# Sparse attention and an FFN on one core: in the last quarter VectorE transposes half of the weights in 32x32 blocks, and the rest of the transpose goes through DRAM

## The chip, the core and the metric

The kernel runs on one core of a Trainium2 chip. The core has a matrix engine (TensorE, PE in the profile; its weight loads are the row PEld), a vector engine (VectorE, DVE), a scalar engine (ScalarE, ACT), GpSimd (POOL) and a sync engine (SP) that issues most of the DMAs. Each engine works through its own list of instructions in order and waits for the others by semaphores. The metric is the device time of one execution in microseconds, lower is better.

## The reference

Attention with the 32 largest scores kept, over 8 batches of 8 heads, 576 positions and a head size of 64; then an FFN with an ELU. Cut to what matters:

```python
scores = q @ k.T / 8                       # (8, 8, 576, 576)
kth = the 32nd largest of each row
scores = where(scores >= kth, scores, -1e9)
attn = exp(scores - max); attn = attn / (attn.sum(-1) + 1e-9)
x = (attn @ v), heads side by side         # (4608, 512)
h = x @ w_in                               # (4608, 2048)
g = where(h > 0, h, exp(min(h, 0)) - 1)
out = g @ w_out                            # (4608, 512)
```

All of it is in float32; w_in and w_out come in as float64 and are decoded on the chip in the first steps.

## The kernel before

The attention is cut into 144 steps. A step is 128 queries of one batch and one pair of heads (or 64 remaining queries of two pairs), with all 576 keys: a score tile `sc` of 128 x 2 x 576. A batch has 18 steps: 16 ordinary ones and two for the remaining queries, which come last in an even batch and first in an odd one. Four ordinary steps (two remaining ones) make one tile of tokens over all eight heads.

What a step does, by engine: TensorE multiplies q and k (`scores`, L331, matmuls at L348) and ScalarE copies the product into `sc` (L368). VectorE looks for the 32nd largest value of each row: `first_max` (L373) finds eight, and three calls of `next_max` (L377) each replace the eight found (L379) and find the next eight (L385). GpSimd pushes the scores below the 32nd far down (`mask`, L397 to L399), ScalarE takes the exponential and its sum `den` (`exp`, L435). Then the weights have to be transposed so that TensorE can multiply them with v: `trans` (L464) makes nine TensorE transposes through PSUM (L475, eight, and L493, one), and ScalarE copies them into `et` (L480, L494). `attend` (L496, matmuls at L508) multiplies `et` with v into `av`. At the end of a tile, `invert` (L440) adds EPS to the sums (L444), takes the reciprocal (L445), transposes it in small (L446), and spreads it over the partitions by way of DRAM (L450, L456, L462); `normalise` (L520) multiplies with it on GpSimd (L523).

The steps overlap. In iteration n of the loop VectorE works on step n; mask and exponential belong to step n-1, the transpose to step n-2. In even iterations TensorE first computes the scores of step n+2, then attends for the steps n-4 and n-3, then computes the scores of step n+3. `et` has two buffers, one for even and one for odd steps; `sc` has seven. k and q of a step are loaded by `load_kq` (L328) from a DRAM copy of their transposed form, four steps ahead. That form is made once for each batch and pair of heads: the pairs 4 to 19 are loaded by `load_qk` (L228, L234), transposed by TensorE in the iterations that `turns` names (L682 to 686; `transpose_qk`, L299, L307) and stored by `keep_kq` (L322); the last twelve pairs are transposed by VectorE in 32x32 blocks (`transpose_blocks`, L264), in an order that the loads (`load_blocks`, L252, L255) have prepared.

The FFN is fed in pieces between these. The tokens are grouped into blocks of one to three tiles (`sizes`, L623, for each pair of batches). When the last tile of a block is normalised, its pieces join a queue: 32 pieces of the hidden layer (`hidden`, L536, matmuls at L543; ScalarE L557 to L559 and GpSimd L560 make the ELU) and eight for each tile of the projection (`project`, L562, matmuls at L567, copy out at L576, store at L579). `feed` (L600) is called twice in each iteration and issues pieces up to a share of planner's units a step; a piece of the projection counts 1.75, one of the hidden layer 1.33 for three tiles and 0.89 for two. The share is what is left divided by the steps until the next block is due, with a cap (L606): 6.6 in the first half of the steps, 7.2 in the second. What is left at the end is issued after the last step.

The first six steps (`EARLY`) run without this overlap: exponential, transpose, attend and normalise of step n-1 stand in iteration n, and the mask is made by another route (`mask_early`, L401, with the Relu of ScalarE at L423 and a subtraction at L426). In them and in the next few the weights of the FFN are decoded in `decode` slots (L661; VectorE L188 and L189, GpSimd L193, ScalarE L182 and L183).

The order of every engine's instructions is the order in which this program issues them.

Of the kernel before, what the change touches and what calls it, by code (L numbers as in the profile page):

```python
# [16 lines left out]
EPS = 1.0e-9  # L17
# [44 lines left out]
def kernel(  # L62
# [313 lines left out]

    def next_max(u, between=None):  # L377
        for i in range(2):
            nc.vector.match_replace(u.wk[:, i, :], u.m[:, i, :], u.cur[:, i, :], TAKEN)  # L379
        u.cur = u.wk  # L380
        if between is not None:
            decode(*between)
        u.m = small.tile([P, 2, 8], FP32, tag="m", name="m")
        for i in range(2):
            nc.vector.max(u.m[:, i, :], u.cur[:, i, :])  # L385
# [14 lines left out]

    def mask_early(u):  # L401

# [13 lines left out]
        for i in range(2):  # L416
            at = slice(i, i + 1)
            nc.gpsimd.tensor_scalar(
                pos[:, at], kth[:, at], neg[:, at], -1.0, ALU.mult, ALU.mult
            )  # L420
        for i in range(2):
            pen, s = u.wk[:, i, :], u.sc[:, i, :]
            nc.scalar.activation(  # L423
                pen, s, AF.Relu, scale=neg[:, i : i + 1], bias=pos[:, i : i + 1]
            )
            nc.gpsimd.tensor_tensor(s, s, pen, ALU.subtract)  # L426
        biases(u, True)

    def exp(u, i):
        g = u.g  # L430
        if g.den is None:
            g.den = small.tile([P, H], FP32, tag="den", name="den", bufs=2)
        at = u.hps[i] if g.rem else i * NHP + u.hps[0]
        s = u.sc[:, i, :]
        nc.scalar.activation(  # L435
            s, s, AF.Exp, bias=u.neg[:, i : i + 1], scale=scale,
            accum_out=g.den[:, at : at + 1],
        )

    def invert(g):  # L440


        n = NHP if g.rem else H
        nc.vector.tensor_scalar_add(g.den[:, 0:n], g.den[:, 0:n], EPS)  # L444
        nc.vector.reciprocal(rec[:, 0:n], g.den[:, 0:n])  # L445
# [18 lines left out]
    def trans(u):  # L464
# [27 lines left out]
        else:  # L492
            nc.tensor.transpose(ps[:, 0, 0:P], e[:, JP : JP + P], ident[:])  # L493
            nc.scalar.copy(half[:, 0, :], ps[:, 0, 0:P])  # L494

    def attend(u):  # L496
        u.attended = True
# [4 lines left out]
        for j, hp in enumerate(u.hps):  # L502
            for c in range(J + 1):
                for i in range(2):
                    r = slice(i * D, (i + 1) * D)
                    at = (j if g.rem else i) * J + c if c < J else 2 * J + j
                    q0 = (i ^ j) * R if g.rem else 0
                    nc.tensor.matmul(  # L508
# [91 lines left out]
    def feed(n, part):  # L600
# [4 lines left out]
        until = next(r for r in dues if r > n) - n  # L605
        share = min(left / until, 6.6 if n < NS // 2 else 7.2)  # L606

# [14 lines left out]
    EARLY = 6  # L622
    sizes = {0: (1, 1, 1, 1, 1, 1, 1, 2), 2: (2, 2, 2, 3), B - 2: (3, 3, 2, 1)}  # L623
    steps, first, order = [], {}, []
# [27 lines left out]
    for n, blk in enumerate(order):  # L652
        blk.over = order[n + 2] if n + 2 < len(order) else None
    NS = len(steps)
    dues = [blk.ready for blk in order] + [NS + 5]

    def sums(u):
        u.summed = True
        invert(u.g)
# [16 lines left out]
    for p, pair in enumerate(pairs):  # L676
# [6 lines left out]
        elif p >= NHP:  # L683
            n = p - 2 if p < NHP + 4 else p - 1
            n = n if n < EARLY + 5 else EARLY + 5 + 2 * (n - EARLY - 5)
            turns[n] = pair
# [18 lines left out]
    with tc.manual_schedule():  # L705
# [20 lines left out]
        for n in range(NS + 4):  # L726
# [39 lines left out]
            if early:  # L766
# [9 lines left out]
                feed(n, 0.5)  # L776
                if last and last.ends:
                    sums(last)
                next_max(now, (n, 3))
                decode(n, 4)  # L780
# [6 lines left out]
                next_max(now, (n, 5))  # L787
                if last and last.ends:
                    normalise(last.g)
                mask_early(now)  # L790
                decode(n, 6)
# [8 lines left out]
            if last:  # L800
                if n > EARLY:
                    mask(last, 1)
                exp(last, 0)
            if done and not done.turned:
                trans(done)
# [50 lines left out]
```

## Time and profile before

| | |
|---|---|
| median of 3 runs | 1649.95 us (1649.19 to 1651.17) |
| the profiled execution | 1647.37 us, of which its span 1644.3 |
| TensorE busy | 1577.9 us, 96% of the span |
| VectorE busy | 1476.5 us, 90% |
| GpSimd, ScalarE busy | 1142.4 and 914.2 us |
| transposes of the weights on TensorE (L475), 1152 | 151.4 us busy |
| their copies by ScalarE (L480), 144 | 144.7 us |
| DMA queue of SP and ScalarE | 166400 packets, 172.1 MB |

The span starts with the first instruction. A step starts on VectorE with its first MAX8 of L373: step 4 at 68.8 us, step 11 at 162.6, step 74 at 794.6, step 108 at 1152.4, and the last one, 143, at 1521.4. An ordinary step without waits takes VectorE 9.6 us. Durations in the profile are those of one instruction and neighbours overlap a little, so sums of steps are taken from start to start. Waits are put down to the instruction that came last.

### The profile page before, as it was taken

How to read it: one execution, taken by the hardware profiler on the slowest of the kernel's cores; microseconds unless marked ns; L12 is line 12 of the kernel's file. 1: busy time of each engine (PE TensorE's matmuls, PEld its weight loads, DVE VectorE, ACT ScalarE, POOL GpSimd, SP SyncE). 2: the span in 40 equal slices, each digit the busy share in tenths (PEclk: the TensorE clock that was granted, in tenths of full speed). 3: DMA queues.
4: the chain of work that ended last, by engine and by line, in shares of the span. 5: the costliest groups of instructions: out<-in, count | busy, mean ns of one | idle time of the engine just before them, and what ended most of it. 6: DMA issues, size and time to landing. Idle time of an engine off the chain costs nothing.

```text
span 1644.3 us, 28759 instructions
## 1 busy us (share of the span) xinstructions
PE 1577.9 (96%) x9928; PEld 1057.7 (64%) x9928; DVE 1476.5 (90%) x3098; ACT 914.2 (56%) x1865; POOL 1142.4 (69%) x1456
## 2 busy tenths in 40 slices
PE   7878999999999999999899999999999999999999
PEld 5665777777675858576565665565565565565565
DVE  7999799999999999999999999989999989989200
ACT  5875566555564646455464574565475475465221
POOL 3777677677786878777687687677687588678321
PEclk9979999999999999999999999999999999999999
DMA  9864454423131413233423524333433312120000
GB/s 312 267 196 130 138 176 141 134 88 118 31 122 46 154 57 115 71 93 92 120 68 104 173 72 128 110 84 107 121 94 118 132 51 89 68 71 14 20 7 13
DMA packets 168914, 174.52 MB, mean 106 GB/s; under 512 B 124225, under 2 KB 132417, under 8 KB 168769
## 3 DMA queue, kind: packets, MB, share of 16 engines
q1 hardware_dynamic: 166400, 172.10, 33.8%
q8 instruction: 78, 1.28, 0.3%
q10 hardware_dynamic: 2368, 0.59, 0.2%
q14 instruction: 68, 0.55, 0.1%
HBM read 144.18 MB, written 28.46 MB: 105 GB/s over the span
## 4 chain that ended last, share of the span: by engine, by line
PE 81%; POOL 6%; DVE 4%; ACT 3%; DMA 3%; issue 2%; SPq 1%; ACTq 0%; DVEq 0%; POOLq 0%
PE ops L567 28%; PE hps L543 27%; PE avps L508 9%; PE scps L348 9%; PE eps L475 6%; POOL sc L399 2%; DVE m L385 2%; DVE wk L379 1%; POOL wk L397 1%; POOL gT L560 1%; DMA w_out<-in_moe_w_in_dram 1%; POOL wk L398 1%; DMA kin<-in_k_dram 1%; PE qkps L299 1%; PE eps L493 1%
## 5 line engine op out<-in xcount | busy, mean ns | idle before, releaser
L385 DVE MAX8 m<-wk 128x8 f32<-128x576 f32 x864 | 609.1, 746 | 0.0
L543 PE MATMUL hps<-xT,w_in 128*128 128x128 f32 (+2 forms) x2432 | 535.3, 376 | 13.8 <-POOL xT L523 10.2
L567 PE MATMUL ops<-w_out,gT 128*128 128x512 f32 x1152 | 519.8, 596 | 8.3 <-ACT osb L576 8.3
L543 PEld LDWEIGHTS hps<-xT,w_in 128*128 128x128 f32 x2432 | 385.4, 195 | 138.8 <-issue 19.4
L379 DVE MATCH_REPLACE8 wk<-m,wk 128x576 f32<-128x576 f32 x576 | 423.1, 742 | 0.0
L399 POOL TENSOR_TENSOR sc<-sc,wk 128x576 f32<-128x576 f32 x276 | 389.1, 1410 | 23.0
L567 PEld LDWEIGHTS ops<-w_out,gT 128*128 128x128 f32 x1152 | 209.6, 190 | 243.0 <-issue 213.2
L435 ACT ACTIVATE sc<-sc,neg 128x576 f32<-128x576 f32 x288 | 224.1, 778 | 224.1 <-POOL sc L399 222.0
L560 POOL TENSOR_TENSOR gT<-gT,n 128x384 f32<-128x384 f32 (+1 forms) x168 | 187.6, 1121 | 180.8 <-ACT n L559 178.3
L368 ACT COPY sc<-scps 128x576 f32<-128x576 f32 x287 | 169.4, 641 | 115.4 <-PE scps L348 113.3
L397 POOL TENSOR_SCALAR wk<-sc,nth 128x576 f32<-128x576 f32 x276 | 206.2, 747 | 26.9
L379 DVE MATCH_REPLACE8 wk<-m,sc 128x576 f32<-128x576 f32 x288 | 211.6, 742 | 0.0
L373 DVE MAX8 m<-sc 128x8 f32<-128x576 f32 x288 | 200.8, 738 | 0.3 <-issue 0.2
L348 PE MATMUL scps<-kq 64*128 64x288 f32 (+3 forms) x1344 | 182.3, 420 | 19.4 <-ACT sc L368 9.3
L398 POOL TENSOR_SCALAR wk<-wk 128x576 f32<-128x576 f32 x276 | 184.0, 667 | 22.8
L480 ACT COPY et<-eps 128x1024 f32<-128x1024 f32 x144 | 144.7, 1005 | 76.8 <-PE eps L475 75.2
L508 PE MATMUL avps<-et,vE 128*64 128x128 f32 (+1 forms) x3200 | 175.5, 265 | 5.4 <-ACT et L480 3.4
L508 PEld LDWEIGHTS avps<-et,vE 128*64 128x64 f32 x3200 | 158.1, 137 | 32.2 <-issue 24.2
L475 PEld LDWEIGHTS eps<-ident,sc 128*128 128x128 f32 x1152 | 133.4, 141 | 56.4 <-issue 36.5
L557 ACT ACTIVATE n<-hps 128x384 f32<-128x384 f32 (+1 forms) x168 | 90.3, 537 | 136.7 <-PE hps L543 132.7
L348 PEld LDWEIGHTS scps<-kq 64*128 64x128 f32 (+1 forms) x1344 | 102.4, 176 | 88.9 <-issue 33.4
L475 PE MATMUL eps<-ident,sc 128*128 128x128 f32 x1152 | 151.4, 274 | 6.8 <-ACT sc L435 2.9
(73 smaller groups left out, 963.6 us busy)
## 6 DMA issues: line engine op xcount, KB each, us to landing
kq<-kqd SPq DMA_DIRECT2D x152, 576.0 KB
kqd<-kq SPq DMA_DIRECT2D x32, 576.0 KB
rb<-recd SPq DMA_DIRECT2D x64, 128.0 KB
out_dram<-osb SPq DMA_DIRECT2D x32, 256.0 KB
kin<-in_k_dram SPq DMA_DIRECT2D x18, 256.0 KB
qin<-in_q_dram SPq DMA_DIRECT2D x17, 256.0 KB
w_out<-in_moe_w_in_dram SPq DMA_DIRECT2D x2, 2048.0 KB
vE<-in_v_dram SPq DMA_DIRECT2D x32, 128.0 KB
```

The costliest lines, as they stand in the source:

```text
L348: nc.tensor.matmul(ps[rows, j, at : at + keys.stop - keys.start], u.kq[hp][r, 1, q0 : q0 + g.ql], u.kq[hp][r, 0, keys], start=True, stop=True,
L373: nc.vector.max(u.m1[:, i, :], u.sc[:, i, :])
L379: nc.vector.match_replace(u.wk[:, i, :], u.m[:, i, :], u.cur[:, i, :], TAKEN)
L385: nc.vector.max(u.m[:, i, :], u.cur[:, i, :])
L397: nc.gpsimd.tensor_scalar(pen, s, u.nth[:, i : i + 1], 2.0**100, ALU.add, ALU.mult)
L399: nc.gpsimd.tensor_tensor(s, s, pen, ALU.add)
L435: nc.scalar.activation(s, s, AF.Exp, bias=u.neg[:, i : i + 1], scale=scale, accum_out=g.den[:, at : at + 1],)
L475: nc.tensor.transpose(ps[:, i, c * P : (c + 1) * P], e[:, k0 + c * P : k0 + (c + 1) * P], ident[:],)
L508: nc.tensor.matmul(g.av[r, hp, 0:ql], vE[g.b, hp][:, i, (c + i) % (J + 1), :], u.et[:, at, q0 : q0 + ql], start=(c == 0), stop=(c == J),)
L543: nc.tensor.matmul(ps[:, f % G, :], w_in[:, i, f * P : (f + 1) * P], blk.xT[:, i, 0:N], start=(i == 0), stop=(i == NC - 1),)
L560: nc.gpsimd.tensor_tensor(g, g, n, ALU.subtract)
L567: nc.tensor.matmul(blk.o[:], blk.gT[f // NG][:, f % NG, s * P : (s + 1) * P], w_out[:, f, :], start=(f == 0), stop=(f == NF - 1),)
```

## The change

In the last quarter of the steps (from `LATE`, step 108) the even ordinary steps no longer use `trans`. `trans_blocks` lets VectorE transpose the 128 x 1152 tile in place in 32x32 blocks, stores it to DRAM (one DMA of 590 KB), and reads it back into `et` with four DMAs that put the blocks in their places, each in pieces of 32 floats (128 bytes). `attend` takes the chunks of those steps by their new positions. In iteration n the VectorE instruction stands after the first `next_max`, and the five DMAs on SP's queue.

Beside that:

- from step 108 the cap of `feed` is 8.0 instead of 7.2;
- the last two batches are grouped into blocks of 2, 2, 2, 2 and 1 tiles instead of 3, 3, 2 and 1;
- EPS is added by ScalarE, in `exp` of a tile's last step, instead of by VectorE in `invert`;
- in the first six steps the reciprocals of a tile come two instructions and a decode later in VectorE's list, the bias of the exponential is computed before the Relu instead of after the subtraction, and `normalise` comes after those small operations instead of before them;
- the q/k pairs 12 to 19 are transposed two steps later (13, 15 ... 27 instead of 11, 13 ... 25), and the loads that follow each transpose move with it.

```diff
-    def next_max(u, between=None):
+    def next_max(u, between=None, done=None):
         for i in range(2):
             nc.vector.match_replace(u.wk[:, i, :], u.m[:, i, :], u.cur[:, i, :], TAKEN)
         u.cur = u.wk
         if between is not None:
             decode(*between)
+        if done is not None and done.ends:
+            sums(done)
...
-    def mask_early(u):
+    def mask_early(u, between=None):
...
+        biases(u, True)
+        if between is not None:
+            between()
         for i in range(2):
             pen, s = u.wk[:, i, :], u.sc[:, i, :]
             nc.scalar.activation(
                 pen, s, AF.Relu, scale=neg[:, i : i + 1], bias=pos[:, i : i + 1]
             )
             nc.gpsimd.tensor_tensor(s, s, pen, ALU.subtract)
-        biases(u, True)
...
+        if u.ends and i == 1:
+            den = g.den[:, 0 : NHP if g.rem else H]
+            nc.scalar.activation(den, den, AF.Copy, bias=EPS)
...
-        nc.vector.tensor_scalar_add(g.den[:, 0:n], g.den[:, 0:n], EPS)
...
+    def trans_blocks(u):
+        u.turned = True
+        e = u.sc[:].rearrange("p i s -> p (i s)")
+        nc.vector.transpose(e, e)
+        u.et = spare_tile(u.n % 2, "et").rearrange("p (c q) -> p c q", q=P)
+        d = dram.tile([P, 2 * S], FP32, tag="e", name="ed", bufs=2)
+        nc.sync.dma_start(d[:], e)
+        for a in range(4):
+            qs = slice(32 * a, 32 * (a + 1))
+            nc.sync.dma_start(
+                u.et[:, 0 : 2 * J + 1, qs],
+                d[qs, :].rearrange("k (c b q) -> b k c q", b=4, q=32),
+            )
...
+                    if u.n in by_blocks:
+                        at = i * (J + 1) + c if c < J else J
...
-        share = min(left / until, 6.6 if n < NS // 2 else 7.2)
+        share = min(left / until, 6.6 if n < NS // 2 else 7.2 if n < LATE else 8.0)
...
-    sizes = {0: (1, 1, 1, 1, 1, 1, 1, 2), 2: (2, 2, 2, 3), B - 2: (3, 3, 2, 1)}
+    sizes = {0: (1, 1, 1, 1, 1, 1, 1, 2), 2: (2, 2, 2, 3), B - 2: (2, 2, 2, 2, 1)}
...
+    LATE = 3 * NS // 4
+    by_blocks = {u.n for u in steps[LATE:] if u.n % 2 == 0 and not u.g.rem}
...
-            n = n if n < EARLY + 5 else EARLY + 5 + 2 * (n - EARLY - 5)
+            n = n if n < EARLY + 5 else EARLY + 7 + 2 * (n - EARLY - 5)
...
-                if last and last.ends:
-                    sums(last)
-                next_max(now, (n, 3))
+                next_max(now, (n, 3), last)
...
-                if last and last.ends:
-                    normalise(last.g)
-                mask_early(now)
+                tile_ends = last and last.ends
+                mask_early(now, (lambda: normalise(last.g)) if tile_ends else None)
...
-            if done and not done.turned:
+            if done and done.n in by_blocks:
+                trans_blocks(done)
+            elif done and not done.turned:
                 trans(done)
```

## The prediction

> **What bounds the kernel now.** I read the page's slices first, then the waits by stage, then the chain, and last the rows that price the new operations.
>
> ```profile
> PE   7878999999999999999899999999999999999999
> DVE  7999799999999999999999999989999989989200
> DMA  9864454423131413233423524333433312120000
> ```
>
> From slice 5 on TensorE (PE) and VectorE (DVE) are both nearly full; VectorE stops at 1531 us, and TensorE works alone for the last three slices. Which of them paces is seen from the busy time by stretch (columns: us, then busy time of PE, PEld, DVE, ACT, POOL):
>
> ```profile
> 200.00:800.00 600.00, 591.18 (x4210) 427.21 (x4209) 598.16 (x1270) 348.20 (x698) 455.42 (x588) 1.00 0.31 100
> 1152.00:1531.00 379.00, 373.43 (x2162) 225.34 (x2163) 358.65 (x755) 210.68 (x451) 276.05 (x356) 1.00 0.26 82
> ```
>
> Up to 800 VectorE has 1.8 us free in 600: it paces. In the last 36 steps (108 to 143, starting at 1152) it has 20 us free, and TensorE 5.6, nearly all of it short waits for ScalarE: TensorE paces. TensorE's waits early, and where it runs dry at 770 to 850:
>
> ```profile
> PE qkps L299 <- DMA kin<-in_k_dram: 3.5, 1, 3.5
> ...
> PE hps L543 <- POOL xT L523: 4.5, 1, 4.5
> PE scps L348 <- ACT et L480: 1.4, 1, 1.4
> ```
>
> The first is at 164 us, step 11, where a q/k transpose waits for its load; the others are where the FFN ran out of ready blocks and had to wait for step 71's tile. The chain in the last quarter shows what one weight transpose costs TensorE, and the tail what it still owes after the last step:
>
> ```profile
> 1475.90 0.87 PE eps L475 x8
> 1476.78 0.11 PE eps L493
> 1476.88 6.45 PE hps L543 x20
> ...
> 1556.15 27.63 PE hps L543 x128
> 1583.78 13.75 PE ops L567 x32
> ...
> 1612.18 14.29 PE hps L543 x128
> ```
>
> **The change, part by part.** The condition names sixteen steps by my count (even, 108 to 142, without 124 and 126), though the change speaks of 15; I use 16.
>
> *Transposes off TensorE.* 16 x (0.87 + 0.11) = 15.7 us less on the engine that paces there. ScalarE loses 16 x (1.00 + 0.27) = 20 us of et copies, off the path.
>
> *Block transpose on VectorE.* The nearest row is the pair of 128x576 transposes that VectorE already makes:
>
> ```profile
> 1191.48 0.76 DVE L264 STREAM_TRANSPOSE kq<-kbl 128x576 f32<-128x576 f32 x1
> 1192.17 0.73 DVE L264 STREAM_TRANSPOSE kq<-qbl 128x576 f32<-128x576 f32 x1
> 1192.83 0.72 DVE L373 MAX8 m<-sc 128x8 f32<-128x576 f32 x1
> ```
>
> Both take 1.35 us start to start, so 128x1152 takes 1.35 (upper end 2 x 0.76 = 1.52): 16 x 1.35 = 21.6 us (to 24.3). Steps 108 to 143 take VectorE 379 us, 359 of them busy. Minus 4.6 us of EPS additions (below) plus 21.6 gives 376. From its end to the end of the last attend (1552.5) passed 21.4 us, so VectorE's path is 397 us. TensorE's list over the same steps was 1552.5 - 1153.7 = 399; it loses 15.7 and gains 28 by the larger feed (below): 411. TensorE stays longer by 14. If VectorE kept its 20 us of waits for GpSimd, its path would be 417, 6 more: bounds 0 and +6, taken +2, since those waits came from a TensorE that fed late. The transpose waits for the second exponential of step n-2; against the place where it will stand (4.2 us into step n), in the traced even steps that came 1 to 6 us early, except before 124 (1.2 late) and 136 (2.1 late): inside the +6. Behind it on VectorE stand this step's last two selection rounds, and GpSimd's mask waits for those.
>
> *The way through DRAM.* Five DMAs on SP: one write of 590 KB, then, when it has landed, four reads of 1152 packets of 128 bytes. What the reads feed is attend, two steps later. Deadline: the transpose ends 4.2 + 1.35 = 5.5 us into step n; two steps are 21.0 us now (17 pairs from 1153.7 to 1510.1) and about 21.4 then, and the attend starts 1.2 us into its own, so 17 us remain. The write: 590 KB at 47.6 us of engine time a MB (fitted to the key loads of 700 to 1250 us) is 1.8 us on 16 engines, plus 2 to land (the recd write took 2.16): 3.8. First read issue 0.6. A packet of 128 bytes is seen nearly alone in one window, 733 to 744 us:
>
> ```profile
> q1 hardware_dynamic: 2104, 0.27, 15.4%
> ```
>
> 0.154 x 16 x 11 us / 2104 = 12.9 ns of one engine; 4608 of them are 59 us of engine time, 3.7 us spread over 16. Landed by 3.8 + 0.6 + 3.7 + 2 = 10 us: 7 us to spare, cost 0. The other end is the kin row of step 11, where a load behind other traffic took 7.4 us; kin and qin are 2304 packets, so twice that is 14.8 us, landed by 21, 4 us late. The lateness would push the attends back, and the next key loads (2 x 590 KB, 3.5 us), write and reads line up behind one another: 14.8 + 3.5 + 1.8 + 2 + 0.6 = 22.7 us a pair against 21.4, 16 x 1.3 = 21 us. Bounds 0 and +21. Per packet kbl is nearest, per instruction (1024 packets) kin: I take +5, nearer the lower end, because TensorE already starts 0 to 5 us behind VectorE in half the pairs. On SP, what stands behind the waiting write are output stores, whose buffer is wanted again only after 14 us of projection, and at odd steps the reciprocals: no charge.
>
> The Trainium skill, "DMA: Bandwidth & Descriptors", section "Why a DMA increments its semaphore by 16 and not by 1", speaks against this: a hardware-generated DMA uses the largest number of engines up to 16 that divides the outermost dimension on both sides, and the reads' source starts with a dimension of 4. By that rule the reads take 59 / 4 = 14.9 us, and the sum would stand at the +21 end; by the kbl row it would stand at 0. No DMA of the trace has so short an outermost dimension, so no row shows it.
>
> *Feed.* 0.8 more units in each of 36 steps is 28.8 units, about 28 us (a projection piece of 1.75 units takes 1.72 us), moved from the tail into the steps: no change of TensorE's sum. The smaller blocks (ready at 118, 126, 134, 142 instead of 122, 134, 142) keep the queue from running dry at that rate.
>
> *Smaller last blocks.* Hidden layer per 128 rows: 13.8 us in a block of two (27.63 / 2) and 13.76 in a block of three (7.74 us for 24 of 128 matmuls); six tiles change, +0.4. The same stores and output copies.
>
> *EPS on ScalarE.* VectorE's addition takes 0.15 us, but up to 1.3 when GpSimd is at work:
>
> ```profile
> 75.15 1.26 DVE L444 TENSOR_SCALAR den<-den 128x8 f32<-128x8 f32 x1 [1.17 <-ACT sc L435]
> 152.38 0.14 DVE L444 TENSOR_SCALAR den<-den 128x8 f32<-128x8 f32 x1
> ```
>
> From the start of each addition to that of its reciprocal, summed over those between 100 and 800 us, is 7.4 us; over the last 36 steps the 4.6 used above. ScalarE pays 40 x 0.23 (its copy of 128x32), half idle.
>
> *First steps.* Step 4: the reciprocals go behind two match_replaces and a decode, so the 1.17 wait and the 1.29 go: 2.4 us; their six DMAs now follow that decode's weight load on SP (0.3 us), and normalise, 8 us later, found rb landed. The six early masks: neg is computed while GpSimd waits 0.75 us for the Relu anyway, and step 4's normalise comes some 2 us later; its block's FFN does so too, and that early VectorE paces: 0. q/k pairs 12 to 19 go from steps 11, 13 ... 25 to 13, 15 ... 27, with 2 us of TensorE, two ScalarE copies, four loads and one store on SP each; first use is step 54. Pair 12 then has three steps for its load and the 3.5 us wait goes; at its new places the queue is as it was. VectorE's stall after it (5.75 us at 179) goes too.
>
> By step 74 VectorE is 2.4 + 5.75 + 7.4 = 15.5 us earlier. TensorE can follow by 2.4 + 3.5 and by the 4.5 + 1.4 it waited around 800: 11.8 us. If that cover is not there (TensorE late by other work), only the 5.9 remain; nothing at all if a later q/k load stalls instead. Bounds -15.5 and 0, taken -11.8. After 850 TensorE paces and keeps it.
>
> *Sum:* -15.7 + 2 + 5 + 0.4 - 11.8 = -20.1. The profiled execution took 1647.4 (span 1644.3 and 3.1 around it): 1627.3. The median shown stands 2.6 higher: 1629.9, so 1630.
>
> **Rivals.**
> 1. *The early gain is lost.* TensorE is as full as VectorE up to 770, which speaks for it; its two long waits against. 1630 + 11.8 = 1642.
> 2. *Slower: the reads queue up.* Place: the attend that waits for et in each pair of steps. It has eaten the gain when a pair grows by (15.7 + 11.8 - 0.4 - 2) / 16 = 1.6 us above 21.4, and shows as slower from 1.8. At the +21 end the time is 1646, hardly a gain; from there each further microsecond of the reads costs 16: reads of 18 us would end at 1697. For it: four times 1152 small packets, and nothing in the trace that reads so. Against: the price of a packet alone, and two steps of time.
> 3. *VectorE becomes the bound.* Its path 417 against 411, and 24.3 instead of 21.6: 1630 - 2 + 9 = 1637. For: 20 us free against 21.6 added. Against: the tail shrinks by 28 us, so a later end of the steps is covered.
>
> **Numbers.** Forecast 0.50 (own range 1618 to 1636), rival 1 0.14, rival 3 0.13, rival 2 0.23, half of it slower and a third within. 0.2% is 3.3 us, about what a measurement of this kernel can tell from no change. Faster 0.81, same 0.08, slower 0.11. The range: from 1616 (both DMA and VectorE free, the early gain 15.5, rounded up) to 1650 (rival 2's lower half).
>
> **What would show it.** eps of L475 down to 1024 matmuls; a 128x1152 transpose at 1.35 us, 16 times; no wait for kin at step 11; VectorE at step 74 some 15 us earlier; a tail after the last attend of 60 us instead of 88; attend waiting for a DMA by less than 1 us a pair. Wrong if attend waits for et in every pair, or if TensorE's waits at 800 come back elsewhere.

## The result, and the profile after

| | median, us | runs, us | against the kernel before beside it |
|---|---|---|---|
| before | 1649.57 | 1648.79 to 1651.17 | |
| after | 1664.28 | 1660.13 to 1665.82 | 1.0084 [1.0062, 1.0106] |

The change costs 14.7 us, where the forecast was 20 us of gain. The profiled execution of after took 1665.72 us, span 1663.9. Its slices (busy tenths of TensorE, VectorE and the DMA engines):

```profile
PE   7878999999999999999999999999889979988999
DVE  7999999999999999999999989999899778889800
DMA  9874555421213222223334433333544542443310
```

Up to about slice 28 (each is 41.6 us) nothing is worse than before. From there TensorE and VectorE both have holes, and the DMA engines have more to do. By stretch, with the columns of the earlier table (us, busy time of PE, PEld, DVE, ACT, POOL, granted clock, DMA share, GB/s), 200 to 800 us and the last 36 steps up to the end of VectorE's last one:

```profile
200.00:800.00 600.00, 591.30 (x4145) 426.80 (x4144) 593.16 (x1252) 349.24 (x711) 455.34 (x584) 0.99 0.32 103
1144.50:1573.00 428.50, 388.43 (x2181) 254.24 (x2180) 373.31 (x760) 193.11 (x407) 274.29 (x348) 0.96 0.42 114
```

In the last steps TensorE is free for 40 us in 428.5 and VectorE for 55. Neither paces: both wait. The steps 108 to 143 start 417.9 us apart from first to last (1144.5 to 1562.4); before it was 368.9 (1152.4 to 1521.4). TensorE's waits from 1130 us on (us in total, times, longest):

```profile
PE avps L532 <- DMA et<-ed: 34.6, 8, 9.3
PE ops L591 <- ACT osb L600: 4.1, 6, 0.7
```

The attend (L532) waits for the reads into `et`, 34.6 us in all, which no row of before has. The chain of waits goes through one such pair, from the DMA that writes the first turned tile to DRAM up to its attend (start, us, what):

```profile
1180.41 2.81 DMA ed<-sc
...
1183.27 0.61 SPq L513
...
1183.94 2.66 SPq L513
...
1186.65 2.66 SPq L513
...
1189.35 6.82 DMA et<-ed
...
1196.30 3.83 PE avps L532 x40
```

The write lands in 2.81 us. The four reads then follow one another on SP's queue, and from the second on each holds SP for 2.66 us; the attend begins 15.9 us after the write. That is not all of it. The transpose itself, on VectorE, had ended much earlier:

```profile
1168.18 1.36 DVE L507 STREAM_TRANSPOSE sc<-sc 128x1152 f32<-128x1152 f32 x1
```

It ended at 1169.54, and the write was issued at 1180.41. SP's queue in those 10.9 us (start, us, line, operation, count; a few of its rows):

```profile
1169.47 0.60 SPq L280 DMA_DIRECT2D vE<-in_v_dram  x1
...
1173.81 1.06 SPq L328 DMA_DIRECT2D kq<-kqd  x2
1174.91 0.62 SPq L252 DMA_DIRECT2D qbl<-in_q_dram  x1
...
1180.00 0.31 SPq L255 DMA_DIRECT2D qbl<-in_q_dram  x1
1180.41 0.37 SPq L510 DMA_DIRECT2D ed<-sc  x1
1183.27 8.72 SPq L513 DMA_DIRECT2D et<-ed  x4
1192.10 2.67 SPq L603 DMA_DIRECT2D out_dram<-osb  x1
```

SP hardly waited (0.5 us for a load of `kq`): it issued the loads of v, k and q that stand ahead of the write in its list, some 0.6 us each. So there are three parts to the lateness: the queue ahead of the write, the write, and the reads. Over the sixteen pairs, the write is issued 0 to 13.3 us after the transpose (mean 3.6), the first read 2.85 to 9.3 us after the write (mean 5.7; for the one of 8.96, at 1246.51, a store of `kqd` and two loads of `kq`, 590 KB each, had been issued in the 3.8 us before), and the reads hold SP some 8.7 us; in the pair above the last one lands 4 us after that. In the eight pairs where the attend waited, it began 20.0 to 32.5 us after the transpose.

The chain's end is better than before:

```profile
1597.18 6.24 PE hps L567 x28
1603.43 13.75 PE ops L591 x32
...
1631.84 14.29 PE hps L567 x128
1646.13 13.75 PE ops L591 x32
```

From the last attend (to 1597.2) there are 62.7 us until TensorE's last matmul at 1659.88; before, 88.

### The profile page after: what moved, and what is told of

Read it like the earlier page. It is cut to its first block, busy times and chain, and to the rows that moved or that the text cites. A ratio compares the mean times of both kernels' runs of the same rounds, so it can differ in the third digit from the quotient of the medians.

```text
span 1663.9 us, 28799 instructions
## 1 busy us (share of the span) xinstructions
PE 1570.2 (94%) x9912; PEld 1076.9 (65%) x9912; DVE 1483.2 (89%) x3074; ACT 899.6 (54%) x1849; POOL 1140.1 (69%) x1448
## 4 chain that ended last, share of the span: by engine, by line
PE 68%; DVE 10%; DMA 7%; POOL 5%; SPq 4%; ACT 3%; issue 3%; DVEq 0%; POOLq 0%; ACTq 0%
PE hps L567 23%; PE ops L591 22%; PE avps L532 9%; PE scps L348 7%; PE eps L481 5%; DVE wk L379 4%; DVE m L387 4%; DMA et<-ed 3%; SPq L513 2%; DMA ed<-sc 2%; POOL sc L401 2%; DMA w_out<-in_moe_w_in_dram 1%; POOL gT L584 1%; POOL wk L399 1%; PE qkps L299 1%
## 5 line engine op out<-in xcount | busy, mean ns | idle before, releaser
L567 PE MATMUL hps<-xT,w_in 128*128 128x256 f32 (+2 forms) x2560 | 534.1, 365 | 15.8 <-POOL xT L547 10.2
L567 PEld LDWEIGHTS hps<-xT,w_in 128*128 128x128 f32 x2560 | 408.8, 194 | 122.4 <-issue 19.8
L584 POOL TENSOR_TENSOR gT<-gT,n 128x512 f32<-128x512 f32 (+1 forms) x160 | 187.1, 1174 | 218.1 <-ACT n L583 215.4
L399 POOL TENSOR_SCALAR wk<-sc,nth 128x576 f32<-128x576 f32 x276 | 206.2, 747 | 26.9
L532 PE MATMUL avps<-et,vE 128*64 128x128 f32 (+1 forms) x3200 | 184.3, 272 | 40.3 <-DMA et<-ed 34.6
L532 PEld LDWEIGHTS avps<-et,vE 128*64 128x64 f32 x3200 | 166.7, 142 | 66.6 <-issue 57.2
L348 PE MATMUL scps<-kq 64*128 64x288 f32 (+3 forms) x1344 | 182.2, 420 | 18.6 <-ACT sc L368 10.6
L486 ACT COPY et<-eps 128x1024 f32<-128x1024 f32 x128 | 128.6, 1005 | 79.9 <-PE eps L481 78.3
L581 ACT ACTIVATE n<-hps 128x512 f32<-128x512 f32 (+1 forms) x160 | 88.9, 556 | 132.2 <-PE hps L567 129.7
L481 PEld LDWEIGHTS eps<-ident,sc 128*128 128x128 f32 x1024 | 118.6, 141 | 43.5 <-issue 30.8
L481 PE MATMUL eps<-ident,sc 128*128 128x128 f32 x1024 | 133.5, 273 | 3.0 <-ACT sc L368 1.8
```

Source lines behind the costliest of these rows:

```text
L348: nc.tensor.matmul(ps[rows, j, at : at + keys.stop - keys.start], u.kq[hp][r, 1, q0 : q0 + g.ql], u.kq[hp][r, 0, keys], start=True, stop=True,
L399: nc.gpsimd.tensor_scalar(pen, s, u.nth[:, i : i + 1], 2.0**100, ALU.add, ALU.mult)
L481: nc.tensor.transpose(ps[:, i, c * P : (c + 1) * P], e[:, k0 + c * P : k0 + (c + 1) * P], ident[:],)
L532: nc.tensor.matmul(g.av[r, hp, 0:ql], vE[g.b, hp][:, i, (c + i) % (J + 1), :], u.et[:, at, q0 : q0 + ql], start=(c == 0), stop=(c == J),)
L567: nc.tensor.matmul(ps[:, f % G, :], w_in[:, i, f * P : (f + 1) * P], blk.xT[:, i, 0:N], start=(i == 0), stop=(i == NC - 1),)
L584: nc.gpsimd.tensor_tensor(g, g, n, ALU.subtract)
```

## The experiments

Twelve kernels, in three groups of four. Each group has its own runs of the kernel before: 1648.38, 1647.24 and 1647.44 us; where two kernels of different groups are compared, up to 1 us can come from that. The theories: **A**, the way through DRAM is late, because reads with a short outermost dimension go on few DMA engines; against it **A2**, that 128-byte packets are slow on whichever engines, **B**, that VectorE becomes the bound, and **D**, that the larger feed or the smaller blocks cost the time.

### All but the block transposes: e1_no_blocks

```diff
-    by_blocks = {u.n for u in steps[LATE:] if u.n % 2 == 0 and not u.g.rem}
+    by_blocks = set()
```

> The changed kernel with no step transposed in blocks (all weights go through TensorE); feed, block sizes, EPS and first steps as changed. Theory A (the loss is the way through DRAM: four reads that each hold SP 2.66 us and land late) and theory B (the loss is VectorE's 1.3 us in the middle of the selection) both expect the last 36 steps back to some 369 + 28 us and the early 8 us kept: 1640 to 1644. Theory D (feed cap and smaller blocks lose by themselves): 1655 or more.

1634.39 us, 0.9915 [0.9901, 0.9930]. The block transposes with their DMAs cost 30 us; everything else in the change together is a gain of 14. D falls.

### The same reads, cut by key block: e2_outer32

The four reads move the same bytes in the same packets of 128 bytes between the same places; only the order of the dimensions is another, so that the outermost one is 32 (keys) instead of 4 (blocks).

```diff
-        for a in range(4):
-            qs = slice(32 * a, 32 * (a + 1))
+        src = d[:].rearrange("(a k) (c b q) -> b k c a q", a=4, b=4, q=32)
+        for b in range(4):
+            ks = slice(32 * b, 32 * (b + 1))
             nc.sync.dma_start(
-                u.et[:, 0 : 2 * J + 1, qs],
-                d[qs, :].rearrange("k (c b q) -> b k c q", b=4, q=32),
+                u.et[ks, 0 : 2 * J + 1, :].rearrange("k c (a q) -> k c a q", a=4),
+                src[b],
             )
```

> The changed kernel with the four reads cut by key block instead of by query block: same packets, bytes and number of DMAs, but the outermost dimension on both sides is 32 instead of 4 and 128. Theory A1 (few DMA engines serve a read whose outermost dimension is 4): a read holds SP 0.6 us instead of 2.66, et lands some 10 us after the transpose, attend no longer waits: 1624 to 1632. Theory A2 (128-byte packets are slow on any engines): reads still 2 us and more each, 1655 to 1665. Theory B (VectorE): 1655 to 1665, with reads of 0.6 us.

1621.47 us, 0.9836 [0.9821, 0.9850]: 43 us faster than the changed kernel, 27 faster than before. A holds, and A2 and B fall: the packets are the same, and VectorE does the same. A packet costs the same too. The DMA queue in the changed kernel from 1187 to 1192 us and in this one from 1185 to 1189, while the reads run (packets, MB, share of sixteen engines):

```profile
q1 hardware_dynamic: 2108, 0.27, 34.2%
```

```profile
q1 hardware_dynamic: 3789, 0.48, 76.2%
```

That is 13.0 and 12.9 ns for a packet, the forecast's own figure (share x 16 x time / packets); what differs is how many packets are under way at a time. The reads on SP's queue (duration in ns: least, median, most), first of the changed kernel and then of this one:

```profile
L513 SPq DMA_DIRECT2D et<-ed x64: 522/2657/3335, 1183.3 to 1586.6; - x64
```

```profile
L514 SPq DMA_DIRECT2D et<-ed x64: 557/736/1796, 1184.5 to 1541.7; - x64
```

TensorE's waits from 1130 us on (the two largest) have no row for `et` any more:

```profile
PE ops L592 <- ACT osb L601: 4.1, 6, 0.7
PE hps L568 <- ACT gT L583: 2.4, 2, 1.3
```

### VectorE's part alone: e3_vector_only

The write and the reads are left out; `attend` takes the `et` of two steps before.

```diff
-        u.et = spare_tile(u.n % 2, "et").rearrange("p (c q) -> p c q", q=P)
-        d = dram.tile([P, 2 * S], FP32, tag="e", name="ed", bufs=2)
-        nc.sync.dma_start(d[:], e)
-        for a in range(4):
...
+        u.et = steps[u.n - 2].et
```

> The changed kernel without the five DMAs: VectorE still transposes in the 16 steps, attend takes the transposed weights of an earlier step (so the output is not the reference's). Theory A: nothing to wait for, 1622 to 1632. Theory B: VectorE's price alone, 1655 to 1665.

1620.33 us (1617.21 to 1621.03), 0.9827 [0.9812, 0.9842]. Without these DMAs the kernel is about 1 us from the one with the well-cut reads, and the runs of the two overlap. So the way through DRAM need not cost anything that shows; as it was written it cost 43 us.

### The first steps alone: e4_first_steps

EPS on ScalarE, the small moves of the first steps and the later q/k turns; no block transposes, the cap of 7.2 and the sizes 3, 3, 2, 1 as before.

```diff
-        share = min(left / until, 6.6 if n < NS // 2 else 7.2 if n < LATE else 8.0)
+        share = min(left / until, 6.6 if n < NS // 2 else 7.2)
...
-    sizes = {0: (1, 1, 1, 1, 1, 1, 1, 2), 2: (2, 2, 2, 3), B - 2: (2, 2, 2, 2, 1)}
+    sizes = {0: (1, 1, 1, 1, 1, 1, 1, 2), 2: (2, 2, 2, 3), B - 2: (3, 3, 2, 1)}
...
+    by_blocks = set()
```

> Only EPS on ScalarE, the moved small operations of the first steps and the q/k pairs two steps later; transposes, feed and blocks as before. The profile of the changed kernel has VectorE 8 us earlier at steps 74 to 108. If that is kept to the end: 1640 to 1643. If TensorE's later waits eat it: 1648 to 1650.

1637.25 us, 0.9930 [0.9914, 0.9947]: 11.1 us of gain, where the forecast had 11.8. The feed and the sizes without the block transposes are then worth only 2.9 us (1637.25 to 1634.39, with runs that overlap).

### Reads cut further: e5_outer2

Each read of the changed kernel in two, so that eight reads of 576 packets have an outermost dimension of 2.

```diff
+            src = d[qs, :].rearrange("k (c b q) -> b k c q", b=4, q=32)
+            for h in range(2):
-            nc.sync.dma_start(
-                u.et[:, 0 : 2 * J + 1, qs],
-                d[qs, :].rearrange("k (c b q) -> b k c q", b=4, q=32),
-            )
+                nc.sync.dma_start(
+                    u.et[64 * h : 64 * (h + 1), 0 : 2 * J + 1, qs],
+                    src[2 * h : 2 * h + 2],
+                )
```

> The changed kernel, each of its four reads cut in two by query block, so that the outermost dimension of a read is 2 and there are eight reads of 576 packets a pair. Theory 1 (the outermost dimension sets on how many engines a read goes, and each packet of 128 B costs an engine and the issuing queue some 9 ns): each of the eight reads has 288 packets on each of 2 engines, as a read of four had on 4, so each still holds SP about 2.66 us, a pair's reads 21 us where they took 10.6, and the time goes up by some 16 pairs x 10 us less what slack is left, to between 1700 and 1830 us. Theory 2 (the price is of packets, on whichever engines): a read has half the packets, holds SP about 1.3 us, and the time stays at about 1664 us (1658 to 1672).

1824.23 us, 1.1070 [1.1054, 1.1087]: theory 1. A read of half as many packets holds SP as long as the whole one did, and a pair's eight hold it for 19.7 us instead of 8.7:

```profile
L515 SPq DMA_DIRECT2D et<-ed x128: 504/2666/3081, 1183.3 to 1744.9; - x128
```

```profile
1183.33 19.72 SPq L515 DMA_DIRECT2D et<-ed  x8
1203.16 2.56 SPq L605 DMA_DIRECT2D out_dram<-osb  x1
```

If 576 packets go on 2 engines and 1152 on 4, each engine has 288 packets, and 2.66 us is 9.2 ns a packet in both. The DMA engines agree: while these reads run (1186 to 1202 us) they are busy 17% of sixteen at 27 GB/s, half of the 34% and 54 GB/s of the changed kernel, and 13.0 ns a packet again. (Packets of one engine can overlap: in e2 the share reaches 106% from 1187 to 1191 us. So the shares do not give the number of engines itself; that it halves with the dimension does not hang on that.) The number of partitions that a read writes does not order the three kernels: 64 here, 128 in the changed kernel, 32 in e2, which is the fastest. This kernel is 160 us slower than the changed one for 11.0 us more of reads in each of 16 pairs: 14.5 of each 16 us come through to the end.

### Poor reads that nobody waits for: e10_aside

The kernel e2, with the four poor reads issued once more behind the good ones, into a DRAM tile.

```diff
+        aside = dram.tile([P, 2 * J + 1, P], FP32, tag="aside", name="aside", bufs=2)
+        for a in range(4):
+            qs = slice(32 * a, 32 * (a + 1))
+            nc.sync.dma_start(
+                aside[:, :, qs],
+                d[qs, :].rearrange("k (c b q) -> b k c q", b=4, q=32),
+            )
```

> The kernel with the reads cut by key block (1621.5 us), and behind the four good reads of each pair the four reads of the changed kernel once more, into a DRAM tile that nothing reads. The output is whole. Theory 1 (the loss is et's lateness: TensorE waits for the four reads): et is on time, the poor reads hold SP 10.6 us a pair with nothing near behind them, and the time stays within 1619 to 1627 us. Theory 2 (the loss comes as well from what the poor reads hold up: SP's queue, with the loads of k, v and the weight blocks behind them, or the engines that they fill): the time is between 1635 and 1664 us, with waits for those loads at TensorE.

1714.08 us, 1.0403 [1.0387, 1.0418], beyond both expectations. `et`'s reads are good here, and still the kernel is 93 us slower than e2. GpSimd waits for the reciprocals on their round trip through DRAM, TensorE waits for `et`:

```profile
POOL xT L555 <- DMA rb<-recd: 93.6, 8, 21.0
PE avps L540 <- DMA et<-ed: 32.7, 9, 8.3
```

The queue shows why `et` can be late with good reads: the write of a pair stands behind the poor reads of the pair before and all that they held up.

```profile
1184.24 10.72 SPq L521 DMA_DIRECT2D aside<-ed  x4
1195.06 3.63 SPq L611 DMA_DIRECT2D out_dram<-osb  x1
...
1207.18 0.31 SPq L255 DMA_DIRECT2D kbl<-in_k_dram  x1
1207.59 0.37 SPq L510 DMA_DIRECT2D ed<-sc  x1
```

That write's transpose had ended at 1188.90, 18.7 us earlier. Over the sixteen pairs the write goes out 13.0 us after the transpose on average; 3.6 in the changed kernel, 1.7 in e2. So a read with few engines has two costs, its own lateness and that of everything behind it. Whether that waits on SP's queue or on the DMA engines, this run does not tell apart. How the 43 us of the changed kernel divide between them this run can't say: its extra reads hold SP 3.3 us each, not 2.66, go to DRAM and come on top of the good ones, and in the changed kernel the reciprocals cost GpSimd only 1.7 us.

### Block transposes without the feed and the sizes: e6_old_feed

Kernel e2 with the cap and the sizes of before (the first two edits of e4).

> The kernel with the reads cut by key block (1621.5 us), with the feed-forward work of the last quarter at the old bound of 7.2 a step and the last blocks at the old sizes 3, 3, 2, 1. Theory 1 (TensorE is freed by 1 us a step and the step shortens by itself; the feed only shortens the tail): 1623 to 1628 us, 2 to 6 us of which are the tail. Theory 2 (a step is paced by VectorE, and freed TensorE time counts only when it is filled): the time goes back to 1632 to 1638 us, as without the block transposes. Theory 3 (the feed and sizes do nothing): 1619 to 1623 us.

1634.86 us, 0.9913 [0.9894, 0.9932]: theory 2. The block transposes without the feed are worth 2.4 us (e4 to e6, 1.3 if each is counted from the kernel before of its own group; the runs overlap), the feed and the sizes without the transposes 2.9 (e4 to e1), and both 15.8 (e4 to e2). The traces say where it goes, by TensorE's attend group (times in ns, then the start of the first and of the last one); in this order the kernels e4, e1, e6 and e2:

```profile
L532 PE MATMUL avps<-et,vE x3200: 221/272/474, 38.7 to 1544.7; 128*64 128x128 f32 x149, 128*64 128x64 f32 x40
```

```profile
L532 PE MATMUL avps<-et,vE x3200: 221/272/475, 38.7 to 1563.7; 128*64 128x128 f32 x149, 128*64 128x64 f32 x40
```

```profile
L533 PE MATMUL avps<-et,vE x3200: 221/273/473, 37.4 to 1543.7; 128*64 128x128 f32 x149, 128*64 128x64 f32 x40
```

```profile
L533 PE MATMUL avps<-et,vE x3200: 221/272/325, 37.4 to 1554.0; 128*64 128x128 f32 x149, 128*64 128x64 f32 x40
```

| profiled execution | last attend starts | from there to the end of the span |
|---|---|---|
| before | 1552.2 | 92.1 |
| e4: first steps | 1544.7 | 92.1 |
| e1: first steps, feed, sizes | 1563.7 | 67.0 |
| e6: first steps, block transposes | 1543.7 | 92.1 |
| e2: all, well-cut reads | 1554.0 | 67.0 |
| after: all, poor reads | 1596.9 | 67.0 |

The feed and the sizes take 25.1 us from the tail and put that work into the steps. Without the block transposes the steps get 19.0 us longer for it, with them 10.3. The block transposes alone shorten the steps by 1.0 us: TensorE has less to do, but in its place VectorE, with 1.36 us more in almost every second step, mostly sets their length. In the last 36 steps TensorE has 5.4 us free in 378.0 and VectorE 24.3 in e4; in e6 it is 15.6 and 9.3 in 381.1, and 6.9 of TensorE's are three waits for `et`. So each half of the change needs the other.

### EPS on VectorE again: e9_eps_back

Kernel e2, with the addition where it was.

```diff
-        if u.ends and i == 1:
-            den = g.den[:, 0 : NHP if g.rem else H]
-            nc.scalar.activation(den, den, AF.Copy, bias=EPS)
...
+        nc.vector.tensor_scalar_add(g.den[:, 0:n], g.den[:, 0:n], EPS)
```

> The kernel with the reads cut by key block (1621.5 us), with EPS added by VectorE again, as before the change, and not by ScalarE. The forecast put 7.4 us on EPS in the first half; if that stands, 1627 to 1631 us. If VectorE's slack in the first half covers it, as the starts of its steps suggest (8 us gained by step 74, 7 of them by step 14), 1620 to 1624 us.

1622.91 us (1620.86 to 1623.50), 0.9848 [0.9833, 0.9862]: 1.4 us more than e2, with runs that overlap. Step 74 starts at 787.9 instead of 786.9, and from step 14 to 74 this kernel takes 1.9 us more. EPS on ScalarE is worth 1 to 2 us there, not 7. The additions are 6.7 us of VectorE's time between 100 and 800 us, and they do go; but VectorE's waits for GpSimd's mask (196 to 790 us) are 6.1 us in e2, in seven waits, and 1.2 here. Most of what is saved turns into waiting.

### Block transposes from the half on: e11_half_blocks

Kernel e2 with `LATE = NS // 2`: block transposes and the cap of 8.0 from step 72.

> The kernel with the reads cut by key block (1621.5 us), with the block transposes and the bound of 8.0 on the feed from the half of the steps on, and not from the last quarter on: some 32 transposes by VectorE for 16. If each transpose off TensorE is worth what the sixteen were (13 us between the kernel without blocks and this one), another 8 to 13 us: 1608 to 1614. If TensorE is no longer what paces those steps (VectorE's step has 9.6 us without and 10.9 us with a transpose), nothing, or VectorE's 1.35 us of each comes on top: 1619 to 1643 us.

1641.11 us, 0.9962 [0.9947, 0.9977]: 20 us lost against e2. Step 108 starts at 1160.7, 15.6 us later than in e2, so the loss lies in the steps that are newly turned. The stretch 830 to 1144 us, in this kernel and in e12 below, which has neither block transposes nor the higher cap there:

```profile
830.00:1144.00 314.00, 295.29 (x1668) 174.71 (x1667) 303.86 (x616) 162.99 (x358) 225.93 (x296) 0.98 0.56 150
```

```profile
830.00:1144.00 314.00, 309.40 (x1802) 186.68 (x1799) 302.64 (x633) 178.24 (x387) 233.20 (x306) 1.00 0.38 111
```

Without them VectorE has 11.4 us free in 314; the thirteen block transposes in that stretch need 13 x 1.36 = 18 us. A step with one starts 10.87 us before the next, where 9.62 is the rule. VectorE does less of its list in the same time (616 instructions, the transposes among them, for 633), and TensorE is left with 19 us unused: here VectorE is, for the most part, what paces. TensorE also waits for `et`, 12.7 us in five waits between 830 and 1160 us, and 8.6 us in three waits (760 to 1170) for the FFN's next tiles, so not all of the 15.6 us is VectorE's; the shares were not tried apart.

### The old sizes with the new feed: e12_old_sizes

> The kernel with the reads cut by key block (1621.5 us), with the old sizes 3, 3, 2, 1 of the last blocks and the new feed of 8.0. The feed and the sizes together were worth 13 us (1634.9 without either). If the feed carries it, 1620 to 1625 us (the forecast had 0.4 us for the sizes); if the sizes carry it, because the blocks that come due after the last step are what the tail of 88 us is made of, 1630 to 1636 us.

Kernel e2 with the sizes 3, 3, 2, 1. 1632.77 us, 0.9912 [0.9897, 0.9926]: the sizes carry 11.3 of the 13.4 us that feed and sizes are worth beside the transposes. The last attend starts at 1550.6, and the tail behind it is 81.7 us: the higher cap alone takes 10 us from the tail, the earlier blocks another 15. That fits the steps at which the blocks become ready, 118, 126, 134 and 142 instead of 122, 134 and 142; it wasn't tried apart.

### Poor reads in every second pair: e13_half_poor

Kernel e2, with the four reads of the changed kernel wherever the step's number is a multiple of four (eight of the sixteen pairs).

```diff
+        if u.n % 4 == 0:
+            for a in range(4):
+                qs = slice(32 * a, 32 * (a + 1))
+                nc.sync.dma_start(
+                    u.et[:, 0 : 2 * J + 1, qs],
+                    d[qs, :].rearrange("k (c b q) -> b k c q", b=4, q=32),
+                )
+            return
```

> The kernel with the reads cut by key block (1621.5 us), but in every second pair (nine or fewer of the sixteen) the four reads cut by query block, as the changed kernel has them. If each late pair costs the same by itself (43 us over 16 pairs, 2.7 each), 1640 to 1646 us. If a pair between two late ones makes up for one (the steps have slack between the pairs, and the lateness adds up only because it comes each pair), 1622 to 1632 us.

1659.73 us, 1.0077 [1.0061, 1.0092]: half of the poor reads cost 38 of the 43 us. Neither expectation holds. TensorE's waits:

```profile
PE avps L541 <- DMA et<-ed: 31.4, 6, 9.1
```

All six are in pairs with poor reads. In the changed kernel too, 31.9 of its 34.6 us of such waits fall to steps whose number is a multiple of four, and 2.8 to the others. That is not because those pairs have less time by themselves. In e2, where no attend waits for `et`, the attend begins 12.8 to 21.0 us after the end of its transpose: 17.6 on average in the multiples of four, 18.1 in the others. In the changed kernel an attend that waited could have begun after 16 to 23 us in the multiples of four, and after 26 and 28 in the two others. A wait gives the pair behind it time: when the attend of step 108 begins at 1196.3, the transpose of step 110 has long ended, at 1191.4, and its reads run while TensorE is held up; in five of the six waits at multiples of four the next transpose had ended by then. So poor reads in every second pair cost almost as much as in each. This reading is argued from the traces; poor reads in the other pairs alone were not tried.

### The later q/k turns alone: e8_shift_alone

The kernel before with one edit.

```diff
-            n = n if n < EARLY + 5 else EARLY + 5 + 2 * (n - EARLY - 5)
+            n = n if n < EARLY + 5 else EARLY + 7 + 2 * (n - EARLY - 5)
```

> The kernel before with one edit: the turns of q and k from the fifth pair on two steps later. The first steps' edits together gave 11.1 us (1637.3 against 1648.4); EPS alone gave 1.4 us (1622.9 against 1621.5). If the shift carries the rest, by the waits for kin at steps 11 and 12 that it takes away, 1639 to 1643 us; if it is in the other small moves of the first steps (the sums and normalise beside the searches), 1646 to 1650 us.

1641.05 us, 0.9968 [0.9953, 0.9982]: 6.4 us, more than half of what the first steps give. VectorE's and TensorE's waits between 100 and 300 us, before (two of the rows):

```profile
DVE wk L379 <- POOL sc L399: 9.0, 2, 5.8
...
PE qkps L299 <- DMA kin<-in_k_dram: 3.5, 1, 3.5
```

and in this kernel, where no row names `kin`:

```profile
DVE wk L379 <- POOL sc L399: 2.9, 1, 2.9
```

Step 13 starts 5.5 us earlier (182.2 for 187.7), and 4.7 of them are still there at step 74. With EPS (1.4) that leaves some 3 us of the 11.1 for the small moves of the first steps; by the starts of step 74 (787.0 in e4, 7.6 us earlier than before) it is 1 to 2. That is within the spread of the runs, and the moves were not tried alone.

## Why the prediction was wrong

**The step that failed** is "The way through DRAM", where it says "Landed by 3.8 + 0.6 + 3.7 + 2 = 10 us: 7 us to spare, cost 0", and then "I take +5" between 0 and +21. It measured +42.8 (1664.28 against 1621.47). What failed in it is the number of engines that share the reads, and with it the arrival: the price of a packet and the time until the attend were right. The other terms gave -25.1, and the kernel with well-cut reads measured -26.9; that they agree so well is in part luck, as the terms below show. Term by term:

- *The reads.* The forecast's 12.9 ns for a packet held (13.0 in the changed kernel and e5, 12.9 in e2). But it spread the 59 us over 16 engines. They ran on few: with an outermost dimension of 4 the engines were busy for 34% of sixteen, with 2 for 17%, with 32 for 76%. The choice between the price of a packet and that of few engines was put "nearer the lower end", though the reads' shape spoke for the other. The forecast said that no DMA of its trace has so short an outermost dimension; the `recd` writes of the remaining tiles (L450) have one of 4, but with four rows each they price nothing. The Trainium skill, "DMA: Bandwidth & Descriptors", section "Why a DMA increments its semaphore by 16 and not by 1", has the rule on the outermost dimension that the forecast weighed and set aside; e2 and e5 agree with it (a read holds SP 2.66 us with 1152 packets at dimension 4 and with 576 at 2, and 0.74 us at the median with 1152 at 32).
- *SP's queue.* "First read issue 0.6" is right for the first of four, and 2.66 for each of the others: 8.7 us for the four. The forecast then looked only at what stands behind the waiting write ("no charge"). What stands ahead of it, and was not looked at, is the loads of v, k and q at 0.6 us each: up to 13.3 us before the write is issued. In e2 these and the write do no harm: the write goes out up to 11.4 us after the transpose (mean 1.7), the first read 2.8 to 9.6 us after that, and no attend waits.
- *The write.* 3.8 us forecast; 2.85 at the least, 5.7 on average, 7 to 9 in half of the pairs.
- *The deadline.* 17 us from the transpose to the attend was right: 17.9 on average in e2, where nothing holds it up. In the pairs that waited, the attend was ready after 16 to 28 us (its start, less its wait, less the transpose's end), and began after 20 to 32, when the reads had landed; the forecast had them land after 10.
- *The upper bound* of +21 fell too. It took reads of 14.8 us (in the pair shown 12.9 from the first issue to the last landing) and had the cycle of a pair grow by 1.3 us, to 22.7. From step 108 to 143 a pair of steps took 23.9 us (417.9 in 35 steps), in e2 21.7. The queue ahead of the write, and TensorE's slower matmuls after a wait (the last section), were not in it. e5 shows the slope that rival 2 gave: 16 us for each further microsecond a pair, measured 14.5.

**The rivals.** Rival 2 had the mechanism: the attend that waits for `et`, with the condition that a pair grows; 1.8 us above 21.4 was to show as slower, and it grew by 2.5. It had half of its chance on the slower side, 0.11 in all. Rival 1 fell: e4 kept 11.1 of 11.8 us. Rival 3 did not come about in the changed kernel, where VectorE is idle 55 us of 428.5. It holds for the most part where the feed is not raised (e6) and a quarter earlier (e11), in both with some waits for `et`.

**The other terms.** "Transposes off TensorE" 15.7, VectorE's +2 and the blocks' +0.4 make -13.3; measured -15.8 from e4 to e2. But the forecast treated the feed as "no change of TensorE's sum" and so as free of consequence: without feed and sizes the transposes bring 2.4 us. The +0.4 of "Smaller last blocks" priced only their matmuls; in place they are worth 11.3 us, since they let the feed take work from the tail. The forecast names that ("keep the queue from running dry") and gives it no price. The -11.8 of EPS and the first steps is near the measured -11.1 by luck. EPS was 1.4, not 7.4: the additions go, and VectorE waits for GpSimd instead (e9). The 2.4 us of step 4 nearly came (steps 4 to 8 take 62.4 us for 64.3), but step 4 starts 1.8 us later, 70.6 for 68.8, and 69.4 to 71.8 in all kernels with these moves; the forecast had put the early masks at 0. The q/k turns gave 6.4, where the forecast had 5.75 for VectorE and 3.5 for TensorE, and 1 to 3 us are not traced.

**What would show it.** Right: 1024 transposes at L481, the block transpose at 1.36 us, no wait for `kin` at step 11, the tail (62.7 us, forecast 60). Wrong: step 74 is 8.0 us earlier, not 15; the attends wait 34.6 us in eight of sixteen pairs, up to 9.3 in one. TensorE's waits around 800 us did not quite go: 3.5 us for the FFN's next tile are left of 4.5.

## What to carry to other kernels

When a DMA rearranges data, try the order of the loops that gives it a long outermost dimension on both sides (2, 4 and 32 were measured here): the same four reads, with dimension 32 for 4, took 8.7 us of SP's queue down to 3.3 and the kernel from 0.8% slower to 1.6% faster than before. The arrival of a transfer has to be counted from the instruction that makes its data, through all that stands ahead of it on its queue, and set against the time at which the step that uses it is ready. Where two engines pace by turns, relief of one may bring its gain only with work that fills it: in this kernel the transposes and the feed with its smaller blocks each gave under 3 us alone, and 15.8 together.

## What was unexpected in the hardware

**The queue that issues a DMA is held by its packets per engine.** The second to fourth read of a group hold SP 2.66 us, with 1152 packets at an outermost dimension of 4 and with 576 at 2; counted for four and two engines that is 9.2 ns for each packet of one engine. The first holds it 0.6 us: the hold falls on the DMA behind, and the store behind the fourth read holds SP 2.67 us (at 1192.10), where the same store holds it 0.73 in e2. Reads with an outermost dimension of 32 hold it 0.74 us at the median.

**TensorE's clock drops after a wait.** The stretch around the longest wait of the changed kernel (columns as before; the granted clock is the third number from the end):

```profile
1345.00:1349.50 4.50, 0.00 (x0) 0.00 (x0) 4.50 (x9) 0.00 (x0) 3.39 (x4) 0.50 0.50 97
1349.50:1352.00 2.50, 2.46 (x24) 2.49 (x26) 2.50 (x7) 0.00 (x0) 0.00 (x0) 0.50 0.96 269
1352.00:1356.00 4.00, 4.00 (x46) 3.35 (x43) 4.00 (x10) 1.74 (x3) 0.00 (x0) 0.89 0.60 222
1356.00:1360.00 4.00, 4.00 (x20) 3.52 (x19) 1.28 (x3) 1.83 (x6) 0.00 (x0) 1.00 0.16 25
```

From 2.4 us into the wait of 9.3 us until 3.4 us after it the clock is granted by half, and the attend's 40 matmuls take 4.0 us; at full clock they take 2.4. Of the eight waits, the five of 3.0 to 9.3 us have such a stretch, the three of 1.4 to 1.6 us have none; over the last 36 steps the granted clock is 0.96, and 1.00 in e2. Over the kernel the attends are busy 184.3 us, 175.5 in e2: 8.8 us more, nearly all of it in the five attends behind the longer waits, which take 3.7 to 4.5 us; the other whole-pair attends of the last quarter take 2.4. With the 34.6 us of waits that makes 43.4, against the 42.9 us by which the last attend starts later than in e2. So TensorE's waits cost here, all together, about a quarter more than their length. The Trainium skill, "TensorE: Matmul & The Clock Gate", section "Part 1: The HAM clock gate (the "warmup" mystery)", says that the clock goes to half after an idle window of about 3.4 us and returns after as long a busy one; the return agrees, 3.4 us after the wait. The drop comes sooner here: 2.4 us into the longest wait, and after a wait of 3.0 us (ended at 1534.6) too.
